# Two-layer MoE after windowed attention: where a pair's token operand is split between the second products

## The chip, the cores and the metric

The kernel runs on one core of a Trainium2 chip. The metric is the device time of one execution, in microseconds (us). The time before is 720.86 us, the median of three runs (720.2, 720.86 and 722.43).

## The reference

Attention with a window (half the heads plain, half dilated by 4) gives x of 2304 tokens by 512. Then come two layers; the second one is the part in which the change lies:

```python
def _moe_ref(x, w_in, w_out):            # d_ff = 2048
    h = x @ w_in
    g = h - np.tanh(h)
    return (g @ w_out).astype(np.float32)

def _moe2_ref(x, w_in, w_out, g_ln):     # d_ff = 1024
    h = x @ w_in
    h_max = np.max(h, axis=-1, keepdims=True)
    e = np.exp(h - h_max)
    sm = e / (np.sum(e, axis=-1, keepdims=True) + 1e-09)
    solu = h * sm
    mu = np.mean(solu, axis=-1, keepdims=True)
    var = np.mean((solu - mu) ** 2, axis=-1, keepdims=True)
    ln = (solu - mu) / np.sqrt(var + 1e-06) * g_ln
    return (ln @ w_out).astype(np.float32)
```

Every product is made in fp32 accuracy from three products of operands that are split in a high part (fp32r) and a low part (the rest): high by high, high by low, low by high.

## The kernel before, in words

The kernel is scheduled by hand: each engine carries out its instructions in the order in which the program issues them, and waits are put in from the tiles (and the regions of tiles) that an instruction reads or writes.

**Stages.** First the attention units, then the first layer over six groups of 384 tokens (`mm1` at L354, `mm2` at L381). The first layer's result y goes to DRAM (`y_dr`). From about 505 us on, the second layer runs over nine pairs (`NP = 9`) of two tiles of 128 tokens each: pair i holds the odd tile 2i+1 and the even tile 2i.

**Loading and splitting a pair's token operand.** `load_y(j)` (L514) reads 512 KB of y of pair j from DRAM into the one buffer `yr`, issued on SyncE's queue. `split_y(j, parts)` (L519) makes the operand `yt` of the products out of it: seven blocks (four quarters and three sums and differences of quarters, for a Strassen-like scheme with seven products in place of eight), each high and low. It has three parts:

- part 0: three sums on GpSimd into `ysm` (L530), then for blocks 0 and 1 the high part on VectorE (L539, a cast) and the low part on GpSimd (L540);
- part 1: one more sum on GpSimd (L533) into `yr` ahead of part 2, and blocks 4 to 6 out of `ysm`, high on VectorE (L539, 128x768), low on GpSimd (L540, 128x768);
- part 2: blocks 2 and 3 out of `yr`, high on VectorE, low on GpSimd (128x512). With parts (1, 2) the order is L533, then blocks 2 and 3, then blocks 4 to 6.

`yt` has two buffers, `yr` and `ysm` one each. So `load_y(j+1)` waits until split j no longer reads `yr`.

**The products of a pair.** `mm3(i)` (L641) runs seven products on TensorE through `prod` (L617, six matmuls of 128x512 at L622 each), in the order of blocks 0, 5, 4, 6, 3, 1, 2. Between them stand the copy `c` of a PSUM bank on ScalarE (L656), the sums `u2` (L657) and `u3` (L665) on VectorE, and `neg_add` (L638), which makes -h of a tile together with its running minimum. Then the softmax: exp on ScalarE (L688), a product and a mean on VectorE (L693, L699, L700). `fac(t)` (L702) makes the tile's factor: a square with its sum on ScalarE (L706) and seven instructions of one column on GpSimd (L707 to L713). `mm3(i)` ends with the factor of the odd tile; that of the even tile is issued later by the loop.

**The second layer's second product.** `trz(t)` (L715) transposes a tile on TensorE (8 at L723) and splits it (ScalarE L725, VectorE L726). `mm4(t)` (L729) runs 24 matmuls at L736, scales by the factor on ScalarE (L739) and issues the output on SyncE's queue (L740).

**The loop** (L742 to L757) issues `mm3(0)` and `mm3(1)`, then for each i: `mm4` of the odd tile of pair i, `trz` of the odd tile of pair i+1, `fac` of the even tile of pair i+1, `mm4` of the even tile of pair i, `trz` of the even tile of pair i+1, and `mm3(i+2)`. The token operand of pair 2 is split around the loop's first pass (L744 and L751, the rest of it behind `fac(2)`); pair i+1's is split inside `mm3(i)` (L651 and L659), for i of 2 and more, and the next load follows it.

Of the kernel before, what the change touches and what calls it, by code (L numbers as in the profile page):

```python
# [40 lines left out]
def tile_kernel(ctx: ExitStack, tc: tile.TileContext, qk, vw, cst, w_in, w_out, w_in2, w_out2, g_ln, out):  # L41
# [472 lines left out]
    def load_y(j):  # L514
        if j < NP:
            y_raw[j] = p2.tile([128, KD, YT], F32, tag="yr", name=f"yr{j}", bufs=1)
            nc.sync.dma_start(out=y_raw[j], in_=y_dr[:, :, j * YT:(j + 1) * YT])

    def split_y(j, parts=range(3)):  # L519

        if j >= NP:
            return
        r = y_raw[j]
        if 0 in parts:
            y = yt[j] = p2.tile([128, 2, 7, 2, TT], F32R, tag="yt", name=f"yt{j}")
            sm = y_sm[j] = p2.tile([128, 3, 2, TT], F32, tag="ysm", name=f"ysm{j}", bufs=1)
            a11, a21, a22 = r[:, 0:2, 0:TT], r[:, 0:2, TT:YT], r[:, 2:4, TT:YT]
            for o, a, b, op in ((sm[:, 0], a21, a22, ALU.add), (sm[:, 1], sm[:, 0], a11, ALU.subtract),
                                (sm[:, 2], a11, a21, ALU.subtract)):
                nc.gpsimd.tensor_tensor(out=o, in0=a, in1=b, op=op)  # L530
        y, sm = yt[j], y_sm[j]
        if 1 in parts:
            nc.gpsimd.tensor_tensor(out=r[:, 0:2, TT:YT], in0=r[:, 2:4, 0:TT], in1=sm[:, 1], op=ALU.subtract)  # L533
        yh = y[:, 0].rearrange("p s k t -> p (s k) t")
        yl = y[:, 1].rearrange("p s k t -> p (s k) t")
        for p, sl, v in ((0, slice(0, 4), r[:, :, 0:TT]), (2, slice(4, 8), r[:, :, TT:YT]),
                         (1, slice(8, 14), sm.rearrange("p s k t -> p (s k) t"))):
            if p in parts:
                nc.vector.tensor_copy(out=yh[:, sl], in_=v)  # L539
                nc.gpsimd.tensor_tensor(out=yl[:, sl], in0=v, in1=yh[:, sl].bitcast(F32), op=ALU.subtract)  # L540
        if 2 in parts:
            y_raw.pop(j)
            y_sm.pop(j)
# [73 lines left out]
    def prod(ps, y, blk, w, first=True):  # L617

        q = 0
        for kk in range(2):  # L620
            for a, b in ((0, 0), (0, 1), (1, 0)):
                nc.tensor.matmul(ps, y[:, a, blk, kk], w2i[w, kk][:, b], start=first and q == 0, stop=q == 5,  # L622
                                 skip_group_check=not first)
                q += 1

    def bank(pool, tag, i, nm):
        return pool.tile([128, 512], F32, tag=tag, name=f"s{nm}_{i}")

    def neg_add(i, t, n, a, b):

        d = st[2 * i + t]
        if "hn" not in d:
            d["hn"] = p3.tile([128, FF2], F32, tag="hn", name=f"hn{2 * i + t}", bufs=4)
            d["sml"] = p3.tile([128, 8], F32, tag="sml", name=f"sml{2 * i + t}", bufs=6)
            init, acc = 3.0e38, d["sml"][:, 7:8]
        else:
            init, acc = d["sml"][:, 7:8], d["sml"][:, 0:1]
        nc.vector.tensor_tensor_reduce(out=d["hn"][:, n * 512:(n + 1) * 512], in0=a, in1=b, op0=ALU.add, op1=ALU.min,  # L638
                                       scale=-1.0, scalar=init, accum_out=acc)

    def mm3(i, mid=()):  # L641

        y = yt.pop(i)
        for t in range(2):
            st[2 * i + t] = {}
        mid = dict(mid)
        b0, b1 = bank(sa, "b0", i, "p1"), bank(sa, "b1", i, "p6")
        prod(b0, y, 0, "b11")
        prod(b1, y, 5, "t2")
        if i > 1:  # L650
            split_y(i + 1, (0,))  # L651
        u2 = p3.tile([128, 512], F32, tag="u2", name=f"u2_{i}", bufs=1)
        u3 = p3.tile([128, 512], F32, tag="u3", name=f"u3_{i}", bufs=1)
        b2, b3 = bank(sb, "b2", i, "p5"), bank(sb, "b3", i, "p7")
        c = p3.tile([128, 512], F32, tag="c", name=f"c_{i}", bufs=1)
        nc.scalar.copy(out=c, in_=b0)  # L656
        nc.vector.tensor_tensor(out=u2, in0=b1, in1=c, op=ALU.add)  # L657
        if i > 1:
            split_y(i + 1, (1, 2))  # L659
            load_y(i + 2)  # L660
        prod(b2, y, 4, "t1")
        if 0 in mid:
            mid[0]()
        prod(b3, y, 6, "t3")
        nc.vector.tensor_tensor(out=u3, in0=b3, in1=u2, op=ALU.add)  # L665
        neg_add(i, 1, 1, b2, u3)
        b1 = bank(sa, "b1", i, "p4")
        prod(b1, y, 3, "t4")
        neg_add(i, 1, 0, b1, u3)
        if 1 in mid:  # L670
            mid[1]()
        softmax_e(2 * i + 1)
        b3 = bank(sb, "b3", i, "p2")
        prod(b3, y, 1, "b21")
        neg_add(i, 0, 0, b3, c)
        softmax_u(2 * i + 1)
        prod(b2, y, 2, "b22", first=False)
        neg_add(i, 0, 1, b2, u2)
        softmax_e(2 * i)
        softmax_z(2 * i + 1)  # L680
        fac(2 * i + 1)
        softmax_u(2 * i)
        softmax_z(2 * i)

    def softmax_e(i):
        d = st[i]
        d["e"] = p3.tile([128, FF2], F32, tag="e", name=f"e{i}")
        nc.scalar.activation(out=d["e"], in_=d["hn"], func=AF.Exp, bias=d["sml"][:, 0:1], scale=-1.0,  # L688
                             accum_out=d["sml"][:, 1:2])

    def softmax_u(i):
        d = st[i]
        nc.vector.scalar_tensor_tensor(out=d["hn"], in0=d["hn"], scalar=-1.0, in1=d["e"], op0=ALU.mult, op1=ALU.mult,  # L693
                                       accum_out=d["sml"][:, 2:3])
# [7 lines left out]
    def fac(i):  # L702
        d = st[i]
        ssum, ssq, f, half = (d["sml"][:, c:c + 1] for c in (1, 4, 5, 6))
        d["f"] = f
        nc.scalar.activation(out=d["e"], in_=d["hn"], func=AF.Square, accum_out=ssq)  # L706
        nc.gpsimd.memset(half, -0.5)  # L707
        nc.gpsimd.tensor_scalar(out=ssum, in0=ssum, scalar1=1e-9, scalar2=None, op0=ALU.add)
        nc.gpsimd.tensor_tensor(out=ssum, in0=ssum, in1=ssum, op=ALU.mult)
        nc.gpsimd.tensor_scalar(out=ssum, in0=ssum, scalar1=1e-6, scalar2=None, op0=ALU.mult)  # L710
        nc.gpsimd.tensor_scalar(out=ssq, in0=ssq, scalar1=1.0 / FF2, scalar2=None, op0=ALU.mult)
        nc.gpsimd.tensor_tensor(out=ssq, in0=ssq, in1=ssum, op=ALU.add)
        nc.gpsimd.tensor_tensor(out=f, in0=ssq, in1=half, op=ALU.pow)  # L713

    def trz(i):  # L715

        d = st[i]
        z = p3.tile([128, 2, NF2, TT], F32R, tag="z", name=f"z{i}", bufs=3)
        for n in range(2):
            ps = zo.tile([128, 512], F32, tag="zt", name=f"zt{i}_{n}").rearrange("p (j t) -> p j t", t=TT)  # L720
            for j in range(4):
                c = 4 * n + j
                nc.tensor.transpose(ps[:, j], d["hn"][:, c * TT:(c + 1) * TT], ident)  # L723
            zh, zl = z[:, 0, 4 * n:4 * n + 4], z[:, 1, 4 * n:4 * n + 4]
            nc.scalar.copy(out=zh, in_=ps)  # L725
            nc.vector.tensor_tensor(out=zl, in0=ps, in1=zh.bitcast(F32), op=ALU.subtract)  # L726
        d["zt"] = z

    def mm4(i):  # L729
        d = st.pop(i)  # L730
        z = d["zt"]
        po = zo.tile([128, DM], F32, tag="po", name=f"po{i}")
        q = 0
        for j in range(NF2):
            for a, b in ((0, 0), (0, 1), (1, 0)):
                nc.tensor.matmul(po, z[:, a, j], w2o[j][:, b], start=(q == 0), stop=(q == 3 * NF2 - 1))  # L736
                q += 1
        o = p3.tile([128, DM], F32, tag="o", name=f"o{i}")
        nc.scalar.activation(out=o, in_=po, func=AF.Copy, scale=d["f"])  # L739
        nc.sync.dma_start(out=out[i * TT:(i + 1) * TT, :], in_=o)  # L740

    mm3(0)  # L742
    mm3(1, {0: lambda: (trz(1), fac(0)), 1: lambda: trz(0)})
    split_y(2, (0,))  # L744
    for i in range(NP):
        mm4(2 * i + 1)
        if i + 1 < NP:
            trz(2 * i + 3)
            fac(2 * i + 2)
        if i == 0:  # L750
            split_y(2, (1, 2))  # L751
            load_y(3)
        mm4(2 * i)
        if i + 1 < NP:
            trz(2 * i + 2)
        if i + 2 < NP:
            mm3(i + 2)  # L757
# [77 lines left out]
```

## Time and profile before

| | before |
|---|---|
| median of 3 runs | 720.86 us |
| profiled execution | 720.01 us |
| its span, first to last instruction | 718.2 us |
| mean granted TensorE clock | 0.997 |
| TensorE (PE) busy | 697.3 us, 97% |
| VectorE (DVE) busy | 454.9 us, 63% |
| ScalarE (ACT) busy | 367.2 us, 51% |
| GpSimd (POOL) busy | 186.4 us, 26% |

PE stands for matmuls on TensorE and PEld for its weight loads; SP is SyncE. Instructions are named by the line of the kernel that issues them. The start of an instruction counts from the start of the span; a matmul's end is modelled, so its printed length is longer than the distance to the next one, and the distance between starts is what a matmul takes. "Granted clock" is the share of TensorE's full speed (1.00 is 2.4 GHz).

### The profile page before, as it was taken

To read this page: it belongs to the slowest core of one execution; us is meant where nothing else is said; L and a number is where in the kernel's file an instruction comes from. 1 tells how busy PE (TensorE), PEld (TensorE's weight loads), DVE (VectorE), ACT (ScalarE), POOL (GpSimd) and SP (SyncE) were. 2 spreads that over 40 slices of the span, in tenths; PEclk is the share of its full clock that TensorE was granted. 3 is DMA by queue.
4 is the path that set the end of the run, shared out by engine and by line. 5 is a ranking of instruction groups with operands and counts; after the bars stand their busy time and mean duration, and the time that the engine had idled before them with its cause. 6 is when DMAs were issued, how large, how long until landed. Compare 5 with 4: busy or idle time off the path is not lost.

```text
span 718.2 us, 11467 instructions
## 1 busy us (share of the span) xinstructions
PE 697.3 (97%) x4106; PEld 643.9 (90%) x4106; DVE 454.9 (63%) x1157; ACT 367.2 (51%) x917; POOL 186.4 (26%) x253
## 2 busy tenths in 40 slices
PE   6898999999999999999999999999997999999997
PEld 5687999999999999999999999999885888888886
DVE  5988666476677766666767434999564455644550
ACT  5779776465555555555546433656342343334431
POOL 2312311111011111100111102562156545555320
PEclk9999999999999999999999999999999999999999
DMA  9977521232222122322112004633102011110001
GB/s 268 341 255 217 178 78 55 66 111 67 68 65 86 60 67 67 111 67 67 36 65 78 1 1 158 208 119 119 44 16 74 29 59 45 44 60 31 29 16 44
DMA packets 30312, 64.03 MB, mean 89 GB/s; under 512 B 2992, under 2 KB 16816, under 8 KB 30256
## 3 DMA queue, kind: packets, MB, share of 16 engines
q1 hardware_dynamic: 27088, 58.59, 25.9%
q10 hardware_dynamic: 3168, 4.72, 1.8%
q8 instruction: 32, 0.52, 0.3%
q14 instruction: 24, 0.20, 0.1%
HBM read 53.86 MB, written 9.44 MB: 88 GB/s over the span
## 4 chain that ended last, share of the span: by engine, by line
PE 88%; DVE 5%; POOL 2%; DMA 2%; issue 1%; ACT 1%; SPq 0%; POOLq 0%; ACTq 0%; DVEq 0%
PE y L381 28%; PE h L354 28%; PE po L736 12%; PE sp L622 10%; PE pv L281 2%; PE tp L260 2%; PE qkp L205 2%; PE qkp L225 2%; PE zt L723 2%; DVE p L210 1%; DMA qkr<-in_qk_dram 1%; DVE hn L638 1%; DVE wy_wi L129 1%; DMA yr<-y_dr 1%; POOL yt L540 1%
## 5 line engine op out<-in xcount | busy, mean ns | idle before, releaser
L354 PE MATMUL h<-x,wi 128*128 128x384 f32 x1152 | 222.6, 343 | 0.8 <-DVE t L365 0.8
L381 PE MATMUL y<-gs,wo 128*128 128x384 f32 x1152 | 216.8, 338 | 0.0
L354 PEld LDWEIGHTS h<-x,wi 128*128 128x128 f32 x1152 | 200.2, 190 | 2.1 <-DVE t L365 1.0
L381 PEld LDWEIGHTS y<-gs,wo 128*128 128x128 f32 x1152 | 199.0, 188 | 1.8
L253 POOL TENSOR_TENSOR p<-p,rs 96x512 f32<-96x512 f32 x47 | 57.2, 1218 | 351.0 <-DVE rs L251 329.0
L736 PE MATMUL po<-w2o_o,z 128*128 128x512 f32 x432 | 102.6, 394 | 0.0
L365 DVE TENSOR_TENSOR t<-h,t 128x384 f32<-128x384 f32 x96 | 53.0, 552 | 78.2 <-ACT t L362 78.2
L371 DVE TENSOR_TENSOR gs<-t,gs 128x384 fp32r<-128x384 f32 x96 | 82.3, 857 | 23.3 <-ACT gs L368 23.2
L736 PEld LDWEIGHTS po<-w2o_o,z 128*128 128x128 f32 x432 | 80.5, 188 | 17.2
L362 ACT ACTIVATE t<-h 128x384 f32<-128x384 f32 x96 | 46.9, 488 | 92.4 <-PE h L354 89.2
L245 ACT ACTIVATE p<-p,nm 96x128 f32<-96x128 f32 x192 | 75.1, 393 | 21.3 <-DVE nm L210 21.1
L368 ACT CAST gs<-t 128x384 fp32r<-128x384 f32 x96 | 49.0, 510 | 49.9 <-DVE t L365 49.7
L688 ACT ACTIVATE e<-hn,sml 128x1024 f32<-128x1024 f32 x18 | 20.8, 1153 | 72.6 <-DVE sml L638 55.2
L726 DVE TENSOR_TENSOR z<-zt,z 128x512 fp32r<-128x512 f32 x36 | 23.2, 686 | 50.8 <-ACT z L725 50.7
L622 PE MATMUL sp<-w2i_t,yt 128*128 128x512 f32 x216 | 52.4, 397 | 0.8 <-POOL yt L540 0.8
L622 PEld LDWEIGHTS sp<-w2i_t,yt 128*128 128x128 f32 x216 | 40.4, 188 | 10.9 <-POOL yt L540 1.2
L622 PE MATMUL sp<-w2i_b,yt 128*128 128x512 f32 x162 | 42.8, 411 | 3.3 <-DVE u L665 3.3
L622 PEld LDWEIGHTS sp<-w2i_b,yt 128*128 128x128 f32 x162 | 31.0, 196 | 10.4 <-DVE u L665 3.7
L739 ACT ACTIVATE o<-po,sml 128x512 f32<-128x512 f32 x18 | 12.4, 687 | 53.8 <-POOL ysm L530 18.4
L205 PE MATMUL qkp<-qkr 64*96 64x128 f32 x160 | 29.4, 339 | 7.6 <-DMA qkr<-in_qk_dram 6.5
L245 ACT ACTIVATION_READ_ACCUMULATOR p<-p,nm 96x1 f32 x192 | 36.3, 189 | 0.0
L205 PEld LDWEIGHTS qkp<-qkr 64*96 64x96 f32 x160 | 24.1, 206 | 12.3 <-DMA qkr<-in_qk_dram 5.9
(82 smaller groups left out, 827.9 us busy)
## 6 DMA issues: line engine op xcount, KB each, us to landing
qkr<-in_qk_dram SPq DMA_DIRECT2D x28, 448.0 KB, 3.4
raw_wi<-in_w_in_dram SPq DMA_DIRECT2D x16, 511.8 KB, 7.3
raw_wo<-in_w_out_dram SPq DMA_DIRECT2D x16, 511.8 KB, 7.4
v<-in_vw_dram SPq DMA_DIRECT2D x48, 128.0 KB, 3.3
y_dr<-ys ACTq DMA_DIRECT2D x6, 768.0 KB, 3.9
yr<-y_dr SPq DMA_DIRECT2D x9, 512.0 KB, 4.5
out_dram<-o SPq DMA_DIRECT2D x18, 256.0 KB, 2.0
qkr<-in_qk_dram SPq DMA_DIRECT2D x20, 224.0 KB, 5.2
```

Of the source, the lines that this page charges most:

```text
L205: nc.tensor.matmul(ps[:, b], d["r"][:64, b * NQ:(b + 1) * NQ], d["r"][:64, QC + b * NK:QC + (b + 1) * NK], start=True, stop=True)
L245: nc.scalar.activation(out=d["p"][:, b], in_=d["p"][:, b], func=AF.Exp, scale=-1.0, bias=d["nm"][:, b:b + 1], accum_out=d["sm"][:, b:b + 1])
L253: eng.tensor_tensor(out=d["p"], in0=d["p"], in1=d["rs"].unsqueeze(2).to_broadcast([NQ, 4, NK]), op=ALU.mult)
L354: nc.tensor.matmul(ps, w[:, a, k * 128:(k + 1) * 128], xt[g, k][:, b], start=(n == 0), stop=(n == 3 * KD - 1))
L362: nc.scalar.activation(out=t, in_=ps, func=AF.Tanh)
L365: nc.vector.tensor_tensor(out=t, in0=ps, in1=t, op=ALU.subtract)
L368: nc.scalar.copy(out=gs[:, 0], in_=t)
L371: nc.vector.tensor_tensor(out=gs[:, 1], in0=t, in1=gs[:, 0].bitcast(F32), op=ALU.subtract)
L381: nc.tensor.matmul(yb[g][m], wo[c][:, a, m * 128:(m + 1) * 128], gs[:, b], start=(c == 0 and i == 0), stop=(c == NF - 1 and i == 2))
L622: nc.tensor.matmul(ps, y[:, a, blk, kk], w2i[w, kk][:, b], start=first and q == 0, stop=q == 5, skip_group_check=not first)
L726: nc.vector.tensor_tensor(out=zl, in0=ps, in1=zh.bitcast(F32), op=ALU.subtract)
L736: nc.tensor.matmul(po, z[:, a, j], w2o[j][:, b], start=(q == 0), stop=(q == 3 * NF2 - 1))
```

## The change

The split of pair i+2 is issued in pass i of the loop, for all pairs alike: part 0 ahead of `mm4` of pair i's odd tile, parts 1 and 2 behind `trz` of pair i+1's odd tile and ahead of `fac` of pair i+1's even tile, with the load of pair i+3 behind them. The splits inside `mm3` and the special case of the first pass go.

```diff
@@ in mm3 @@
         prod(b0, y, 0, "b11")
         prod(b1, y, 5, "t2")
-        if i > 1:
-            split_y(i + 1, (0,))
         u2 = p3.tile([128, 512], F32, tag="u2", name=f"u2_{i}", bufs=1)
...
         nc.scalar.copy(out=c, in_=b0)
         nc.vector.tensor_tensor(out=u2, in0=b1, in1=c, op=ALU.add)
-        if i > 1:
-            split_y(i + 1, (1, 2))
-            load_y(i + 2)
         prod(b2, y, 4, "t1")
@@ the loop @@
     mm3(0)
     mm3(1, {0: lambda: (trz(1), fac(0)), 1: lambda: trz(0)})
-    split_y(2, (0,))
     for i in range(NP):
+        split_y(i + 2, (0,))
         mm4(2 * i + 1)
         if i + 1 < NP:
             trz(2 * i + 3)
+            split_y(i + 2, (1, 2))
+            load_y(i + 3)
             fac(2 * i + 2)
-        if i == 0:
-            split_y(2, (1, 2))
-            load_y(3)
         mm4(2 * i)
         if i + 1 < NP:
             trz(2 * i + 2)
```

## Rows read from the trace of the kernel before

**Rows 1.** The page, part 1: busy time, share and instructions of each engine.

```profile
PE 697.3 (97%) x4106; PEld 643.9 (90%) x4106; DVE 454.9 (63%) x1157; ACT 367.2 (51%) x917; POOL 186.4 (26%) x253
```

**Rows 2.** Timeline of TensorE: start, us, instruction, count, [idle before it <- releaser].

```profile
526.37 5.67 PE L736 MATMUL po<-w2o_o,z 128*128 128x512 f32 x24
...
541.93 5.47 PE L622 MATMUL sp<-w2i_t,yt 128*128 128x512 f32 x22 [0.78 <-POOL yt L540]
550.67 4.61 PE L622 MATMUL sp<-w2i_b,yt 128*128 128x512 f32 x12 [3.27 <-DVE u L665]
555.12 5.67 PE L736 MATMUL po<-w2o_o,z 128*128 128x512 f32 x24
...
577.66 5.66 PE L736 MATMUL po<-w2o_o,z 128*128 128x512 f32 x24
...
591.81 5.76 PE L622 MATMUL sp<-w2i_t,yt 128*128 128x512 f32 x24
597.41 2.96 PE L622 MATMUL sp<-w2i_b,yt 128*128 128x512 f32 x12
```

**Rows 3.** Windows: length, then PE, PEld, DVE, ACT, POOL busy; granted clock; DMA, GB/s.

```profile
547.40:550.67 3.27, 0.00 (x1) 0.01 (x1) 1.52 (x4) 0.00 (x0) 2.73 (x3) 1.00 0.00 0
550.67:555.12 4.45, 4.45 (x13) 3.56 (x14) 2.92 (x7) 1.24 (x2) 3.56 (x6) 0.62 0.44 120
...
577.66:600.21 22.55, 22.55 (x108) 18.58 (x106) 12.23 (x26) 8.46 (x15) 12.26 (x22) 1.00 0.15 47
```

**Rows 4.** The chain of waits in order of time: start, us, what.

```profile
540.10 4.53 DMA yr<-y_dr
...
545.00 0.70 DVE u L657
...
550.01 0.61 DVE u L665
```

**Rows 5.** Timeline of GpSimd, columns as in Rows 2.

```profile
530.70 0.99 POOL L713 TENSOR_TENSOR sml<-sml 128x1 f32<-128x1 f32 x1
531.67 0.73 POOL L530 TENSOR_TENSOR ysm<-yr 128x256 f32<-128x256 f32 x1
...
533.86 1.30 POOL L540 TENSOR_TENSOR yt<-yr,yt 128x512 fp32r<-128x512 f32 x1
535.10 0.10 POOL L707 MEMSET sml<- 128x1 f32 x1
...
537.26 0.74 POOL L533 TENSOR_TENSOR yr<-yr,ysm 128x256 f32<-128x256 f32 x1
538.53 1.54 POOL L540 TENSOR_TENSOR yt<-yr,yt 128x512 fp32r<-128x512 f32 x1 [0.54 <-DVE yt L539]
540.03 1.85 POOL L540 TENSOR_TENSOR yt<-ysm,yt 128x768 fp32r<-128x768 f32 x1
...
604.83 0.99 POOL L713 TENSOR_TENSOR sml<-sml 128x1 f32<-128x1 f32 x1
```

**Rows 6.** Timeline of TensorE's weight loads, columns as in Rows 2.

```profile
541.93 3.56 PEld L622 LDWEIGHTS sp<-w2i_t,yt 128*128 128x128 f32 x16 [1.21 <-POOL yt L540]
...
614.13 2.05 PEld L622 LDWEIGHTS sp<-w2i_t,yt 128*128 128x128 f32 x9
```

**Rows 7.** Timeline of VectorE, columns as in Rows 2.

```profile
533.33 1.29 DVE L726 TENSOR_TENSOR z<-zt,z 128x512 fp32r<-128x512 f32 x2 [1.72 <-ACT z L725]
...
549.12 0.43 DVE L539 CAST yt<-yr 128x512 fp32r<-128x512 f32 x1 [3.44 <-POOL yr L533]
...
604.64 0.75 DVE L700 TENSOR_SCALAR hn<-hn,sml 128x1024 f32<-128x1024 f32 x1
```

**Rows 8.** Timelines of GpSimd and VectorE around 600 us, columns as in Rows 2.

```profile
599.96 1.25 POOL L708 TENSOR_SCALAR sml<-sml 128x1 f32<-128x1 f32 x1 [1.28 <-ACT e L688]
...
605.94 0.23 POOL L708 TENSOR_SCALAR sml<-sml 128x1 f32<-128x1 f32 x1
...
599.91 1.22 DVE L693 SCALAR_TENSOR_TENSOR hn<-hn,e 128x1024 f32<-128x1024 f32 x1 [0.20 <-ACT e L688]
```

## The prediction, made before the changed kernel was built

> **What bounds the kernel now.** I read the page first: TensorE is busy for 97% of the span [rows 1], so a change to other engines can pay only where TensorE stands still. The timeline of TensorE over the second layer shows where: from 526 us to the end it is idle in two places only, 0.78 and 3.27 us, both in the products of pair 2 [rows 2]. Everywhere later one pass follows the other without a gap. The start of `mm4` of the odd tile marks a pass, and I count from there as T. From T = 555.12 to 577.66 a pass takes 22.54 us, and in the next one TensorE is busy for all of its 22.55 us [rows 2, 3]. The pass from 526.37 to 555.12, the one that holds the products of pair 2, takes 28.75 us [rows 2]. So 28.75 - 22.54 = 6.21 us are lost there, once, and this is all that a better order can win in this stage.
>
> The loss has three visible parts. (a) 0.78 us ahead of the matmul that needs the low part of block 5 of pair 2, released by GpSimd's L540 [rows 2]. (b) 3.27 us ahead of the product of block 3, released by `u3` (L665) [rows 2]. (c) After the second wait TensorE runs slower: in 550.67 to 555.12 its granted clock is 0.62, and the last 12 matmuls of the pass take 4.45 us where the same 12 take 600.21 - 597.41 = 2.80 us one pass later, at clock 1.00 [rows 2, 3]; that is 1.65 us. Together 5.70 us; the other 0.51 us lie in the matmuls around the two waits, whose ends are modelled.
>
> Why (b): the chain of waits goes through the load of pair 3 (issued at 540.10, 4.53 us), then `u2` at 545.00, then `u3` at 550.01 [rows 4]. Both sums are pair 2's and need nothing of pair 3; but pair 3's casts stand ahead of them in VectorE's queue, inside `mm3(2)`, and wait for pair 3's load and for GpSimd: the cast at 549.12 has 3.44 us of idle time before it, released by L533 [rows 7]. The load in turn could only be issued when GpSimd had read `yr` for pair 2, at 538.53 + 1.54 = 540.07 [rows 5].
>
> **The change, part by part.** Nothing is added or taken out. Six splits (pairs 3 to 8) of seven GpSimd instructions and three casts each, and six loads of 512 KB (pairs 3 to 8), move; pair 2's split moves past one factor.
>
> 1. Pair 2's parts 1 and 2 go ahead of `fac(2)` on GpSimd. That factor's seven instructions take from 535.10 to 537.26, 2.16 us [rows 5]. So L533 starts at 535.10, and the last low part ends at 540.03 + 1.85 - 2.16 = 539.72. The weight load that wanted it was ready 1.21 us before 541.93, that is at 540.72 [rows 6]. Wait (a) goes, with 1.0 us to spare: gain 0.78 us and some of the 0.51. The factor itself now ends some 2 us after the split; it is wanted only by `mm4(2)`'s scaling, a pass later, so it costs nothing; without that cover it would cost its 2.16 us. ScalarE's square for it is not moved.
>
> 2. The load of pair 3 can be issued at 540.07 - 2.16 = 537.91 and lands about 4.5 us later, at 542.4. Its split is now wanted not before GpSimd reaches it in the next pass, at T + 5.6 (below), some 12 us later. On SyncE's queue the load now stands ahead of the even tile's output; that output is not ready before `mm4` of the even tile ends, which is a `trz` ahead of block 0, at about T + 12, and the load's wait ends at about T + 11.8 (below), so it holds up nothing; were it late, the output's two buffers would still cover a pass.
>
> 3. Pair 3's casts leave `mm3(2)`. `u2` and `u3` then wait for TensorE alone, as in every later pass. Wait (b) goes, and with it (c). Gain 3.27 + 1.65 us and the rest of the 0.51.
>
> 4. The six splits move from `mm3(i)`, a whole pass before their use, into the pass in which they are used. This is what can go wrong: six times a chain on GpSimd now has a deadline. In a steady pass GpSimd ends the odd tile's factor at 604.83 + 0.99 = 605.82, which is T + 5.6 for T = 600.21 [rows 2, 3, 5]. VectorE's last piece ahead of the new place ends at 604.64 + 0.75 = 605.39, so the cast of part 0 (0.43 us, as the other 128x512 cast in rows 7) does not hold GpSimd up. Then, with durations of pair 2's split, which stood in just this place already (its L530 follows the same L713 [rows 5]): three L530, 533.86 - 531.67 = 2.19 us; L540 of part 0 to the next instruction, 535.10 - 533.86 = 1.24; L533 and the cast behind it to the next L540, 538.53 - 537.26 = 1.27; that L540 to the next, 540.03 - 538.53 = 1.50; the last, 1.85 [rows 5]. Sum 8.05 us: the chain ends at T + 13.66, and reads `yr` for the last time at about T + 11.8. Block 0 is wanted six matmuls of 2.80/12 = 0.23 us ahead of block 5, which starts at 591.81 - 577.66 = T + 14.15 [rows 2], so at about T + 12.7, and is ready at T + 9.0. The deadline is the third weight load of block 5 (the first with a low part): the first one starts at 614.13 - 600.21 = T + 13.92, and the loads follow each other by (2.05 - 0.19)/8 = 0.23 us, so T + 14.38 [rows 6]. There is 0.7 us to spare. I cost the step at nothing; the cover is `mm4` of both tiles. If it were gone, each us of lateness costs six.
>
> 5. VectorE in the new place: the casts of parts 1 and 2 wait for L533 (ends T + 9.8) with the even tile's L726 queued behind them. The odd tile's L726 is over before (it is at 533.33 in pass 0, T + 7.0 [rows 2, 7]), the even one's needs that tile's transposes, which stand right ahead of block 0, so it comes after T + 12. That leaves over 2 us of slack after L533: cost nothing.
>
> Sum: -6.21 us. Against its own time: 720.01 - 6.21 = 713.80 (span 718.2 to 712.0, with 1.8 us around it). The median of the runs is 0.85 above the profiled one, so on that scale 714.65.
>
> The bounds of step 4's cost: below, nothing, since TensorE has no idle time to win there. Above, what VectorE can do to GpSimd. A row shows that it does something: L708 takes 0.23 us alone and 1.25 us beside L693, which reads two tiles of SBUF, and ends when that ends [rows 8]; the L540 of part 2 takes 1.54 against 1.30 for the same shape in part 0 [rows 5]. If everything of VectorE beside the chain shut GpSimd out in full, that would be the two L726 (1.29), the cast of part 0 (0.43) and 0.55 - 0.24 of the 128x768 cast (0.55 estimated as 0.43 x 768/512, less some start cost): 2.0 us, end at T + 15.7, late by 1.3 us in each pass. But in pass 0 the L530 and the L540 that ran beside L726 at 533.33 took 0.73 and 1.30 as listed [rows 5, 7], so I take nothing.
>
> The Trainium skill, page "SBUF — State Buffer", section "Who interferes with whom", says that VectorE and GpSimd share one pair of ports, held for a whole instruction, by a VectorE instruction with two SBUF inputs or by a copy or cast in a two-port mode. Rows 8 agree with the first half. By it the casts alone would count (L726 reads one operand from PSUM): 0.43 + 0.31 = 0.7 us, the chain would end at T + 14.4, just on the deadline, and the time stay 714.65; it makes the margin, not the sum, smaller.
>
> **Rivals.**
> - *The clock or a part of the gap stays.* Something else in `mm3(2)` could be late, as a wait of the small kind (a). For it: TensorE's first gap had another releaser than its second. Against: all sums then wait as in later passes, which have no gap. Price: 1.65 (c) left, 716.3, or 0.78 and 0.51 left, 715.9.
> - *The chain on GpSimd is a little late in each pass*, by 0.3 to 1.0 us: 6 x 0.3 = 1.8 to 6 us given back, 716.5 to 720.7. For: the margin is 0.7 us of 8.05. Against: pair 2's rows are of the same place.
> - *Slower*: the chain is shut out in full, in six passes, at the third weight load of block 5. 6 x 1.3 = 7.8 us, net 1.6 us slower, 722.3; and if each such wait pulls the clock down as the wait of 3.27 us did, another 6 x 1.65 = 9.9 us: 732. It decides against the change from 1.03 us of lateness per pass on (6.21/6), which is 1.75 us more than the rows give.
> - *It does nothing*: if the load of pair 3 weren't what held VectorE. The chain of waits speaks against it: 720.9.
>
> **How the numbers follow.** Forecast 0.82; part of the gap stays 0.06; a little late 0.06, half of it within 0.3%; slower 0.04; nothing 0.02. 0.3% is 2.16 us, about what a measurement of this kernel can tell from no change. Faster 0.82 + 0.06 + 0.03 = 0.91, which I lower to 0.89 for what I have not seen; same 0.07; slower 0.04. The range goes from 713.4 (the sum on the profiled execution, less 0.4 for the scatter of runs) to 717.6 (the first rival, and the second with 0.5 us of lateness per pass).
>
> **What would show it.** Right: no idle time of TensorE in the products of pair 2, a pass of 22.5 us there too, clock 1.00 throughout; the load of pair 3 issued near 538; in later passes the 128x768 L540 ending some 0.7 us before block 5's third weight load; passes of 22.5 us. Wrong: a wait of L622 on L540 that comes six times, passes of over 22.6 us, or L530 and L540 longer than listed.

## The result, and the profile after

The changed kernel takes 715.03 us (median of four runs, 713.84 to 716.65). The kernel before, run beside it, takes 721.64 us (four runs, 720.2 to 722.51). The ratio is 0.9912, with a 95% interval of 0.9884 to 0.9939: 6.6 us or 0.9% faster, and between 4.4 and 8.4 us by the interval. The profiled execution took 715.10 us with a span of 713.3 us.

Lines behind the removed ones move up in the changed kernel: `u2` is L655, `u3` L660, the factor's GpSimd instructions L702 to L708, the transposes L718, their split L720 and L721, `mm4` L731.

First the windows of the changed kernel, the first three passes of the loop and then pair 2's products in two parts, the first 30 matmuls and the last 12 (length; PE, PEld, DVE, ACT, POOL busy; granted clock; DMA share, GB/s):

```profile
527.66:550.21 22.55, 22.55 (x108) 18.59 (x106) 11.93 (x26) 8.46 (x15) 11.66 (x21) 1.00 0.15 47
550.21:572.75 22.54, 22.54 (x107) 18.58 (x106) 12.22 (x26) 8.46 (x15) 12.19 (x22) 1.00 0.15 47
572.75:595.30 22.55, 22.55 (x107) 18.58 (x106) 12.22 (x26) 8.46 (x15) 12.18 (x22) 1.00 0.16 47
540.34:547.41 7.07, 7.07 (x33) 5.73 (x32) 3.15 (x5) 1.70 (x4) 2.38 (x9) 1.00 0.37 111
547.41:550.21 2.80, 2.80 (x14) 2.26 (x12) 1.98 (x7) 1.24 (x2) 0.24 (x1) 1.00 0.02 6
```

The pass with pair 2's products took 28.75 us before [rows 2]; it takes 22.55 us now, like the others. TensorE is busy in all of it, and the last 12 matmuls take 2.80 us at clock 1.00, where they took 4.45 us at 0.62 [rows 3]. So the loss of 6.2 us is gone and no pass has got longer: the seventh ends at 685.49, 7 x 22.55 us behind 527.66. The timeline of TensorE in the same pass shows no idle time at all (start, us, instruction, count; idle time would stand in brackets):

```profile
527.66 5.67 PE L731 MATMUL po<-w2o_o,z 128*128 128x512 f32 x24
...
541.81 5.76 PE L622 MATMUL sp<-w2i_t,yt 128*128 128x512 f32 x24
547.41 2.96 PE L622 MATMUL sp<-w2i_b,yt 128*128 128x512 f32 x12
550.21 5.66 PE L731 MATMUL po<-w2o_o,z 128*128 128x512 f32 x24
```

Before, the 24 matmuls were broken after two by a wait of 0.78 us and the 12 stood behind a wait of 3.27 us [rows 2]. VectorE's timeline shows why the second wait is gone: `u2` and `u3` wait for TensorE alone. The two casts ahead of them are pair 2's own; pair 3's, which held them up before [rows 7], come in the next pass, the first of them at 555.32:

```profile
537.18 0.43 DVE L539 CAST yt<-yr 128x512 fp32r<-128x512 f32 x1 [1.27 <-POOL yr L533]
537.52 0.56 DVE L539 CAST yt<-ysm 128x768 fp32r<-128x768 f32 x1
...
543.48 0.69 DVE L655 TENSOR_TENSOR u<-sp,c 128x512 f32<-128x512 f32 x1 [1.19 <-PE sp L622]
546.21 0.69 DVE L660 TENSOR_TENSOR u<-sp,u 128x512 f32<-128x512 f32 x1 [2.04 <-PE sp L622]
...
555.32 0.42 DVE L539 CAST yt<-yr 128x512 fp32r<-128x512 f32 x1
```

The new chain on GpSimd: its last instruction in the first pass (pair 2), then the chain in the first pass in which a split of pairs 3 to 8 stands there (T = 550.21), then its last instruction in the sixth pass (T = 640.39). Behind it stand the weight loads that need its end in the first two of these passes. The lines are from the timelines of GpSimd and of TensorE's weight loads:

```profile
539.19 1.84 POOL L540 TENSOR_TENSOR yt<-ysm,yt 128x768 fp32r<-128x768 f32 x1
...
554.84 1.00 POOL L708 TENSOR_TENSOR sml<-sml 128x1 f32<-128x1 f32 x1
555.81 0.72 POOL L530 TENSOR_TENSOR ysm<-yr 128x256 f32<-128x256 f32 x1
...
558.01 1.30 POOL L540 TENSOR_TENSOR yt<-yr,yt 128x512 fp32r<-128x512 f32 x1
559.26 0.76 POOL L533 TENSOR_TENSOR yr<-yr,ysm 128x256 f32<-128x256 f32 x1
560.56 1.54 POOL L540 TENSOR_TENSOR yt<-yr,yt 128x512 fp32r<-128x512 f32 x1 [0.54 <-DVE yt L539]
562.06 1.83 POOL L540 TENSOR_TENSOR yt<-ysm,yt 128x768 fp32r<-128x768 f32 x1
...
652.53 1.84 POOL L540 TENSOR_TENSOR yt<-ysm,yt 128x768 fp32r<-128x768 f32 x1
```

```profile
541.58 5.56 PEld L622 LDWEIGHTS sp<-w2i_t,yt 128*128 128x128 f32 x24
...
564.12 5.55 PEld L622 LDWEIGHTS sp<-w2i_t,yt 128*128 128x128 f32 x24
```

The chain ends at 562.06 + 1.83 = 563.89, T + 13.68. The third of the 24 weight loads comes at 564.12 + 2 x 0.233 = 564.59, T + 14.38. There are 0.7 us to spare, and the loads run on without a wait. One pass has less: in the sixth the chain ends at 652.53 + 1.84 = 654.37, T + 13.98, and 0.4 us are left. ScalarE's exp (L683), for which VectorE and then GpSimd wait, begins 0.3 us later there; why it does is not shown.

One thing the two profiles do not share is the time ahead of all this. The first `mm4` begins at 527.66, before at 526.37 [rows 2]. That is why the two profiled executions differ by 720.01 - 715.10 = 4.9 us only, 6.2 less 1.3. The last section shows where the 1.3 us come from.

### The profile page after: what moved, and what is told of

Same layout as the page of the kernel before. It is cut to its first block, busy times and chain, and to the rows that moved or that the text cites. A ratio compares the mean times of both kernels' runs of the same rounds, so it can differ in the third digit from the quotient of the medians.

```text
span 713.3 us, 11466 instructions
## 1 busy us (share of the span) xinstructions
PE 696.0 (98%) x4106; PEld 643.7 (90%) x4106; DVE 455.5 (64%) x1157; ACT 367.2 (51%) x917; POOL 185.9 (26%) x253
## 4 chain that ended last, share of the span: by engine, by line
PE 91%; DVE 5%; issue 1%; ACT 1%; DMA 1%; POOL 0%; SPq 0%; ACTq 0%; POOLq 0%
PE y L381 29%; PE h L354 27%; PE po L731 14%; PE sp L622 12%; PE zt L718 2%; PE pv L281 2%; PE tp L260 2%; PE qkp L225 2%; PE qkp L205 2%; DVE p L210 1%; DVE wy_wi L129 1%; DMA qkr<-in_qk_dram 1%; DVE wi L104 1%; DVE wi L140 1%; POOL p L253 0%
## 5 line engine op out<-in xcount | busy, mean ns | idle before, releaser
L253 POOL TENSOR_TENSOR p<-p,rs 96x512 f32<-96x512 f32 x47 | 57.2, 1218 | 352.3 <-DVE rs L251 330.4
L731 PE MATMUL po<-w2o_o,z 128*128 128x512 f32 x432 | 102.6, 394 | 0.0
L731 PEld LDWEIGHTS po<-w2o_o,z 128*128 128x128 f32 x432 | 80.5, 188 | 17.2
L683 ACT ACTIVATE e<-hn,sml 128x1024 f32<-128x1024 f32 x18 | 20.8, 1155 | 67.0 <-DVE sml L638 50.2
L721 DVE TENSOR_TENSOR z<-zt,z 128x512 fp32r<-128x512 f32 x36 | 23.2, 686 | 35.1 <-ACT z L720 35.0
L622 PE MATMUL sp<-w2i_b,yt 128*128 128x512 f32 x162 | 41.1, 399 | 0.0
L205 PE MATMUL qkp<-qkr 64*96 64x128 f32 x160 | 29.5, 340 | 7.2 <-DMA qkr<-in_qk_dram 5.4
L205 PEld LDWEIGHTS qkp<-qkr 64*96 64x96 f32 x160 | 24.1, 206 | 11.8 <-DMA qkr<-in_qk_dram 5.8
```

The source lines that it names most:

```text
L205: nc.tensor.matmul(ps[:, b], d["r"][:64, b * NQ:(b + 1) * NQ], d["r"][:64, QC + b * NK:QC + (b + 1) * NK], start=True, stop=True)
L253: eng.tensor_tensor(out=d["p"], in0=d["p"], in1=d["rs"].unsqueeze(2).to_broadcast([NQ, 4, NK]), op=ALU.mult)
```

## The experiments

**One part alone: the factor behind the split, in the first pass.** In the kernel before, `fac(2)` moves behind the rest of pair 2's split; all else stays.

```diff
             trz(2 * i + 3)
+            if i == 0:
+                split_y(2, (1, 2))
+                load_y(3)
             fac(2 * i + 2)
-        if i == 0:
-            split_y(2, (1, 2))
-            load_y(3)
```

> The kernel before with one part of the change alone: in the first pass the factor of tile 2 goes behind the rest of pair 2's split and the load of pair 3; all later splits stay inside the products. My theory (the loss in the pass of pair 2's products has two causes: the factor ahead of the split, and pair 3's casts ahead of u2 and u3): wait (a) goes, the load is issued near 538 in place of 540.1 and lands near 542.4, u3 runs near 547.6 and not near 545, so TensorE still waits some 2.2 us for it. That pass takes 24.7 us if the clock stays at 1.00 after the shorter wait, 26.4 us if it falls as before; time 2.4 to 4.0 us below before. Rival (the late load of pair 3 is all of it): the 6.2 us go nearly whole, pass below 23.5 us. Rival (the casts' place is all of it): the pass stays above 27.5 us.

Measured: 718.19 us against 720.65 of before, ratio 0.9969 (0.9950 to 0.9988). In the profile the wait of 0.78 us is gone and the wait for `u3` is 1.87 us. The chain of waits:

```profile
537.65 4.13 DMA yr<-y_dr
...
542.15 0.69 DVE u L657
...
546.64 0.55 DVE yt L539
547.19 0.61 DVE u L665
547.80 0.04 issue
547.85 3.06 PE sp L622 x12
```

It is the chain of [rows 4], with the load begun 2.4 us earlier (0.3 of it because the pass begins earlier): `u2` and `u3` still wait behind pair 3's casts. The pass is 550.75 - 526.07 = 24.68 us at clock 1.00, 4.1 us less than before. So the factor's place is one cause, the casts' place another. Neither rival fits: no one cause is all of it.

The timed gain, 2.5 us, lies in the expected range but is less than the profile's 4.1. The 12 timed runs lie at 715.5 to 715.9 (five) and 717.8 to 721.7 (seven), so I ran the same kernel three times more for its profile.

> The kernel of the first experiment once more, for its profile alone. Its timed runs lie in two groups, near 715.7 and from 717.8 to 721.7, while its one profile (715.65) shows the clock at 1.00 behind the wait of 1.87 us. If the clock falls behind that wait in some executions, a profile of 717 us and more shows a granted clock below 1.00 in the 12 matmuls behind the wait and a pass of 26 us. Rival: the scatter lies ahead of the second layer, the pass is 24.7 us again and the second layer begins later.

> As for the run before it: a second single execution of the same kernel, to see whether the pass of pair 2's products stays at 24.7 us while the time moves.

> As for the two runs before it: a third single execution of the same kernel.

The three, on another chip than the first profile, took 718.45, 718.55 and 717.96 us. The windows of the wait and of the 12 matmuls behind it, in the first and the third of them:

```profile
547.37:549.14 1.77, 0.00 (x1) 0.01 (x1) 1.52 (x4) 0.00 (x0) 1.23 (x2) 1.00 0.00 0
549.14:553.57 4.43, 4.43 (x13) 3.50 (x13) 3.22 (x8) 1.24 (x2) 3.63 (x5) 0.61 0.39 120
```

```profile
548.47:550.13 1.66, 0.00 (x0) 0.00 (x0) 1.51 (x4) 0.00 (x0) 1.12 (x2) 1.00 0.00 0
550.13:553.03 2.90, 2.90 (x12) 2.36 (x13) 2.14 (x6) 1.22 (x2) 2.33 (x3) 1.00 0.32 86
```

The passes are 553.57 - 527.45 = 26.12, 26.15 and 24.48 us. One kernel, one wait: in two executions of four the clock falls behind it (waits of 1.77 and 1.78 us) and 1.5 us more are lost, in two it does not (1.66 and 1.87 us). The expectation had the two as alternatives of theory; they are alternatives of the execution. In all three the second layer also begins 1.4 to 2.5 us later than in the first profile, so both the readings of the scatter hold. They are not all of it: three of the seven longer runs (718.55, 719.63 and 720.46 us) have a mean granted clock of 1.000, so what makes them 3 to 5 us longer is not the clock, and no such execution of this kernel was profiled.

**The factor ahead of the split again, in the first pass.** In the changed kernel `fac(2)` goes back ahead of parts 1 and 2.

```diff
+            if i == 0:
+                fac(2 * i + 2)
             split_y(i + 2, (1, 2))
             load_y(i + 3)
-            fac(2 * i + 2)
+            if i > 0:
+                fac(2 * i + 2)
```

> The changed kernel, but with the factor of tile 2 ahead of parts 1 and 2 of pair 2's split, in the first pass alone. My theory: wait (a) of 0.78 us comes back once, the pass takes 23.6 to 23.7 us in place of 22.5, nothing else changes: 1.1 us over the changed kernel. Rival (the load's start decides): the load is again issued near 540 and pair 3's products are late as well, a second wait in the next pass.

Measured: 716.14 us, ratio to before 0.9947 (0.9927 to 0.9968); 1.1 us over the 715.03 of the changed kernel, which was timed apart from it, so the pass has to decide. In TensorE's timeline the wait is there once and no more:

```profile
541.91 0.63 PE L622 MATMUL sp<-w2i_t,yt 128*128 128x512 f32 x2
543.30 5.39 PE L622 MATMUL sp<-w2i_t,yt 128*128 128x512 f32 x22 [0.76 <-POOL sml L702]
```

The pass takes 551.33 - 527.75 = 23.58 us, the next one 22.55. The load is issued at 541.48, 2.2 us later than in the changed kernel (539.26), and costs nothing. So the place of the factor is worth 1.0 us in this pass, by itself. (The releaser reads L702, a factor's first instruction; it is the next thing on GpSimd behind the L540 whose result block 5 needs.)

**The factor ahead of the split in every pass.**

```diff
+            fac(2 * i + 2)
             split_y(i + 2, (1, 2))
             load_y(i + 3)
-            fac(2 * i + 2)
```

> The changed kernel with the even tile's factor ahead of parts 1 and 2 of the split in every pass. My theory (a chain on GpSimd with 0.7 us to spare): 2.16 us more put it 1.45 us behind the third weight load of block 5, in seven passes; each costs 1.1 to 1.4 us, 8 to 10 us over the changed kernel, 2 to 4 us slower than before. Rival (each wait also brings the clock down as the wait of 3.27 us did): another 1.65 us in each, some 20 us over the changed kernel. Rival (the margin is larger than worked out): a wait in the first pass alone, 1 us.

Measured: 724.35 us, ratio to before 1.0054 (1.0037 to 1.0070): slower than before. The waits of TensorE in the second layer, and two windows of passes:

```profile
PE sp L622 <- POOL sml L702: 7.5, 7, 1.4
```

```profile
525.98:549.55 23.57, 22.81 (x107) 18.49 (x106) 11.93 (x26) 8.46 (x15) 11.64 (x21) 1.00 0.15 45
549.55:573.44 23.89, 22.82 (x108) 18.49 (x106) 12.21 (x26) 8.46 (x15) 12.18 (x22) 1.00 0.14 44
```

Seven waits, as expected. The passes grow by 1.03 us (the first), 1.35 (five) and 1.6 (one): the seven take 693.12 - 525.98 = 167.1 us in place of 7 x 22.55 = 157.8, 9.3 more. By the medians, which were timed apart, it is 724.35 - 715.03 = 9.3, or 10.0 against the 714.32 of the changed kernel's second measurement. The clock stays at 1.00 in these passes. So that the split stands ahead of the even tile's factor is what makes the early place pay at all: moving the casts alone would have lost 3.7 us.

**The load early, the order as before.** In the kernel before, pair 3's tokens get a buffer of their own and are loaded behind the products of pair 0.

```diff
-            y_raw[j] = p2.tile([128, KD, YT], F32, tag="yr", name=f"yr{j}", bufs=1)
+            y_raw[j] = (p3 if j == 3 else p2).tile([128, KD, YT], F32, tag="yr3" if j == 3 else "yr", name=f"yr{j}", bufs=1)
...
     mm3(0)
+    load_y(3)
...
             split_y(2, (1, 2))
-            load_y(3)
```

> The kernel before, but pair 3's tokens go into a buffer of their own and are loaded behind the products of pair 0, some 30 us earlier; the order on GpSimd and VectorE is not changed. My theory (VectorE's casts wait for GpSimd too, which is still at pair 2's split): wait (a) stays, u3 runs near 547.1 in place of 549.9, wait (b) shrinks from 3.27 to some 0.6 us and the clock stays at 1.00: the pass takes 24.2 to 24.6 us, 4.1 to 4.5 us below before. Rival (the load alone): wait (b) goes whole, pass 23.6 us. Rival (GpSimd's queue alone): wait (b) stays over 2 us.

Measured: 716.79 us, ratio to before 0.9949 (0.9933 to 0.9964). TensorE's timeline:

```profile
541.49 5.40 PE L622 MATMUL sp<-w2i_t,yt 128*128 128x512 f32 x22 [0.77 <-POOL yt L540]
547.34 3.07 PE L622 MATMUL sp<-w2i_b,yt 128*128 128x512 f32 x12 [0.44 <-DVE u L665]
```

Both waits are there, the second cut from 3.27 to 0.44 us (0.6 expected), the pass is 550.25 - 525.95 = 24.30 us. The load held up most of the second wait but not all of it: with the tokens there for 30 us, `u3` still stood behind casts that waited 2.3 us for GpSimd's L533. Neither rival fits.

**How much the chain on GpSimd has to spare.** In the changed kernel one, then two sums that nobody uses go into each split.

```diff
+            if i + 2 < NP:
+                scr = p3.tile([128, 256], F32, tag="scr", name=f"scr{i}", bufs=1)
+                r = y_raw[i + 2]
+                for _ in range(1):
+                    nc.gpsimd.tensor_tensor(out=scr, in0=r[:, 0, :], in1=r[:, 1, :], op=ALU.add)
             split_y(i + 2, (1, 2))
```

> The changed kernel with one more sum of 128x256 on GpSimd (its result is not used) ahead of parts 1 and 2 of each split, seven in all, some 0.7 us each. My theory: the chain's 0.7 us to spare are just used up; TensorE waits less than 0.15 us in a pass, passes of 22.5 to 22.7 us, time within 1 us of the changed kernel. Rival (there is more slack than worked out, or less): no trace of it even with two (next run), or waits of 0.3 us and more here already.

> The same with two more sums in each split, some 1.45 us. My theory: 0.7 to 0.8 us behind the third weight load of block 5 in seven passes, each pass 23.1 to 23.3 us, 4 to 5.5 us over the changed kernel. Rival (slack of over 1.5 us): passes stay at 22.5 us. Rival (each wait also costs clock): over 24 us.

Measured with one: 715.55 us; with two: 720.70 us; the changed kernel timed beside them: 714.32 us (last experiment). The second pass of each by the windows:

```profile
550.16:572.74 22.58, 22.58 (x108) 18.48 (x107) 12.22 (x26) 8.47 (x15) 12.93 (x23) 1.00 0.16 46
```

```profile
550.45:573.83 23.38, 22.82 (x108) 18.49 (x107) 12.22 (x26) 8.47 (x15) 13.66 (x24) 1.00 0.15 45
```

The first sum costs at most 0.04 us in six passes and 0.3 in the sixth, the one with 0.4 us to spare; that is 0.4 us, where the medians differ by 1.2, a little over the 1 us expected. The second sum costs 0.80 in the pass shown. In the first kernel the third weight load begins at 564.70, 0.2 us late, and TensorE covers that; in the second one the load waits 1.00 us. So the deadline lies where step 4 put it, and all but at most some 0.15 us of the lateness past it is paid, in every pass: 0.53 in the first pass, 0.84 in five and 1.1 in the sixth make 5.8 us, and the medians differ by 720.70 - 714.32 = 6.4.

**What VectorE can do to the chain.** In the changed kernel a sum of 128x1024 with both inputs in SBUF, that nobody uses, goes behind the odd tile's L721 on VectorE.

```diff
+            if i + 2 < NP:
+                scr = p3.tile([128, 1024], F32, tag="scr", name=f"scr{i}", bufs=1)
+                hn = st[2 * i + 3]["hn"]
+                nc.vector.tensor_tensor(out=scr, in0=hn, in1=hn, op=ALU.add)
             split_y(i + 2, (1, 2))
```

> The changed kernel with one more sum of 128x1024 on VectorE with two inputs from SBUF (its result is not used) behind the odd tile's L721, beside GpSimd's chain, seven in all, 1.2 us each. Theory that such an instruction and GpSimd's shut each other out: a GpSimd instruction beside it (L540 of part 0 or L533) is longer or begins later by 0.4 to 1.2 us, the chain ends at T + 14.1 to 14.9, passes of 22.5 to 23.0 us, 0 to 3.5 us over the changed kernel. Rival (VectorE disturbs GpSimd little): L540 stays at 1.30, L533 at 0.74, the chain ends at T + 13.7, no change in time.

Measured: 716.10 us, 1.8 us over the 714.32 of the changed kernel beside it. The timelines of VectorE and of GpSimd in the second pass:

```profile
558.59 1.29 DVE L721 TENSOR_TENSOR z<-zt,z 128x512 fp32r<-128x512 f32 x2 [1.42 <-ACT z L720]
559.79 2.03 DVE L747 TENSOR_TENSOR scr<-hn 128x1024 f32<-128x1024 f32 x1
```

```profile
558.74 0.74 POOL L530 TENSOR_TENSOR ysm<-yr 128x256 f32<-128x256 f32 x1
559.44 1.30 POOL L540 TENSOR_TENSOR yt<-yr,yt 128x512 fp32r<-128x512 f32 x1
560.69 1.73 POOL L533 TENSOR_TENSOR yr<-yr,ysm 128x256 f32<-128x256 f32 x1
```

They shut each other out: the sum lasts 2.03 us, where L688, also 128x1024 with two inputs from SBUF, takes 1.23; it ends 1.08 us after L540 does, and L533, which takes 0.76 alone, lasts 1.73 and ends 0.6 us after the sum. The pair of L721, which read one operand from PSUM, lengthens nothing: L530 lies wholly beside it and takes 0.74 as elsewhere, and L540, which begins beside it, keeps its 1.30. The chain ends some 1 us later, at 564.45 + 1.85 = 566.30, T + 14.66, and the pass takes 574.39 - 551.64 = 22.75 us: 0.2 us more, and 1.4 us in the seven passes together. This is the page "SBUF — State Buffer" of the Trainium skill, section "Who interferes with whom", in both halves: a VectorE instruction with two SBUF inputs and a GpSimd instruction that reads SBUF exclude each other, one with a single SBUF input and the other operand in PSUM does not.

**The changed kernel once more.**

> The changed kernel once more, without an edit. Its second layer's first mm4 began 1.29 us later in the profile than that of the kernel before, in front of everything the change touches. If that is scatter of single executions, it begins between 526.0 and 527.8 us here; the passes are 22.5 us again, and the time is 5.5 to 7 us below before. Rival (the change delays the first layer): it begins near 527.7 again.

Measured: 714.32 us, ratio to before 0.9903 (0.9879 to 0.9928). The passes are 22.55, 22.54 and 22.55 us again. The first `mm4` begins at 527.74, near the rival's number; but in the changed kernel with the factor first in every pass it begins at 525.98, and in the one without casts moved (the first experiment) anywhere from 526.07 to 528.55. So the change does not delay it; the last section shows what does.

## Why the prediction was right

The forecast was 714.65 us against 720.86, a gain of 6.2 us; the medians give 6.6 with the wide interval above, and the pass that was to change gives 28.75 - 22.55 = 6.20.

- *Where the loss is, and its parts* (what bounds the kernel now): right. The wait of 0.78 us was the factor's place (it alone, put back, costs 1.0 us). The wait of 3.27 us was pair 3's casts in VectorE's queue, which stood there for two things in turn, the load and GpSimd: with the load early 0.44 us are left, with the load 2.2 us earlier in the pass 1.87. The prediction named the wrong product for it: the 12 matmuls behind the wait are those of blocks 1 and 2, and block 1's reuses the bank that `u3` reads; block 3's belongs to the 22 ahead of the wait [rows 2] and needs `u2`. The sum is the same.
- *Step 1*: pair 2's chain was to end 1.0 us ahead of its deadline. It ends at 539.19 + 1.84 = 541.03; the third weight load of block 5 is at 541.58 + 0.47 = 542.05. 1.0 us.
- *Step 2*: the load of pair 3 was to be issued at 537.91. It is at 539.26, and the whole layer begins 1.29 us later, so 537.97 on the same scale. That it lands early is worth nothing in the new order: 2.2 us later cost nothing (second experiment).
- *Step 3*: right; with the waits the slow matmuls went. The prediction counted the 1.65 us of the lowered clock as part of the wait's price. Behind the shorter wait of the first experiment, 1.66 to 1.87 us, the clock fell in two of four executions only. Behind the wait of 3.27 us one execution was profiled, and in it the clock had fallen. That it falls there each time is not shown, but the mean granted clocks speak for it: the kernel before has 0.993 to 0.998 in all 31 timed executions whose clock is on record, where the profiles without any fall have 0.999 or 1.000, those with one 0.997 or 0.998 and those with two 0.995. So the 1.65 us were probably due in each execution, and not luck.
- *Step 4*, the risk: the chain was to end at T + 13.66 against T + 14.38. Measured T + 13.68 and T + 14.38; in the sixth pass, which the rows behind the sum did not cover, T + 13.98. One more sum on GpSimd uses up the 0.7 us, a second one costs some 0.8 us in a pass. The end at T + 14.4, by the casts alone, did not come: the cast of part 0 ends at 555.32 + 0.42 = 555.74, before the chain's first L530 begins (555.81), and what the 128x768 cast costs L540 (1.54 us in place of 1.30) was in the sum already. And a late chain would cost seven passes, not six: pair 2's own is late too when two sums stand in it.
- *Step 5*: the even tile's L721 begins at 563.53, 2.6 us after the last cast ends (560.94); no cost.
- *The rivals*: a late chain did not come, but the runs made it: with the factor ahead of the split in each pass the same move is 3.7 us slower than before. The rival that priced each such wait with a fallen clock (732 us) was too dear: in the profiles of late chains, with waits of 0.25 to 1.4 us, the clock stays at 1.00. No part of the gap stayed.

## What to carry to other kernels

Where an engine at its limit has lost time at one place only, look at what stands ahead of the late instruction in the queue of the engine that releases it: here two sums waited behind casts for the next pair's operand, which waited for a load and another engine. Work for the next step belongs where its inputs have long been there, and a move to a later place is priced by the chain up to its first reader: sum the rows, find the exact instruction that reads the result, and see how much is left, in each pass and not in one. Here 0.7 us were, and 0.4 in one pass, and the order of a 2.2 us factor on the same engine decided between 0.9% faster and 0.5% slower.

## What was not expected of the hardware

The clock of TensorE fell or stayed behind the same idle time, by execution. Besides the wait above there is a place where the first layer's products stand among the attention units: near 58 us (61 in one) TensorE stands still for 2.2 us, waiting for GpSimd's L253, in all thirteen profiles, and behind it the clock fell in eight of them. The windows that follow it, in the changed kernel's profile, and then in the kernel's before:

```profile
58.00:60.00 2.00, 0.16 (x2) 0.16 (x3) 2.00 (x11) 1.59 (x7) 1.78 (x1) 1.00 0.85 265
60.00:62.00 2.00, 2.00 (x11) 2.00 (x11) 0.95 (x5) 2.00 (x8) 0.00 (x0) 0.65 0.69 270
62.00:64.00 2.00, 2.00 (x8) 2.00 (x7) 2.00 (x5) 1.75 (x5) 1.77 (x1) 0.50 0.03 12
```

```profile
58.00:60.00 2.00, 0.00 (x1) 0.00 (x0) 2.00 (x10) 1.60 (x6) 1.74 (x1) 1.00 1.01 239
60.00:62.00 2.00, 1.78 (x12) 1.78 (x13) 0.98 (x4) 2.00 (x9) 0.17 (x1) 1.00 1.03 282
62.00:64.00 2.00, 2.00 (x14) 2.00 (x13) 1.97 (x6) 1.76 (x5) 1.39 (x1) 1.00 0.51 205
```

The 12 matmuls behind it take 63.80 - 60.17 = 3.63 us in the one and 2.17 us in the other. The 12 after them take 2.31 and 2.17 us. Together that is 1.6 us; as the changed kernel came to the place 0.38 us earlier (60.17 against 60.55), some 1.2 of the 1.3 us are left by which its second layer began later, in front of all that was changed. Half the speed (0.50, 1.2 GHz) and full speed (1.00, 2.4 GHz) are the two levels. What decides between them in a given execution stays open; a comparison of two single profiles of this kernel carries some 1.5 us of it for each such place.

The clock is not the only thing that moves the second layer's start. In the profile with the sum on VectorE (717.95 us, mean clock 1.000) the first `mm4` begins at 529.10, 1.4 us later than in the changed kernel, though the clock did not fall near 61 us: TensorE's second and third group of L205 there stand behind waits of 2.54 and 1.79 us for loads (`qkr`), where the changed kernel's profile has 1.11 and 0.81.
